# Smaller MLP tiles in a fused recurrent-attention and MLP kernel: two chunk-batches per tile, attention stages respaced over three PSUM slots, loads reordered

## The chip, the core and the metric

The kernel runs on one core of a Trainium2 chip. The metric is the device time of one execution in microseconds (us), as the median of several runs. Engines are named as in the profile: PE is TensorE's matmul stream and PEld its weight loads, DVE is VectorE, ACT is ScalarE, POOL is GpSimd, and SP is SyncE, whose queue here issues every DMA.

## The reference

The first half is a linear attention with a decaying state for 4 batches, 8 heads, 768 steps and head dimension 48. The second half is an MLP on the 3072 rows of 384 that come out of it.

```
state = 0
for t in range(768):
    cur      = einsum('bhd,bhe->bhde', u * k[t], v[t])
    y[t]     = einsum('bhd,bhde->bhe', r[t], state + cur)
    state    = w[t][..., None] * state + einsum('bhd,bhe->bhde', k[t], v[t])
x = y.transpose(0, 2, 1, 3).reshape(3072, 384)
h = x @ w_in                       # 384 -> 2048
g = s * relu(h)**2 + b
out = g @ w_out                    # 2048 -> 384
```

## The kernel before

Time is cut into six chunks of 128 steps. One chunk of one batch is a *chunk-batch*, numbered n from 0 to 23: n // 4 is the chunk and n % 4 the batch. All work on 128 rows.

**Attention of one chunk-batch.** `load` brings w, r, k and v (four DMAs of 192 KB). ACT takes the logarithm of w (`ln`, L127). PE turns it into running sums with triangular matrices (`cum`, L169 to L177), ACT exponentiates them (`expo`, L191 and L195), and DVE multiplies r and k by them (`mult`, L201, tile prd). PE transposes prd (`trans`, L228, tile trps), and the evacuation out of PSUM is shared: DVE copies one half (L244, RT), ACT the other (L245, KTr). PE forms the matrix of the chunk (`mt`, L255), DVE masks it (`mask`, L267). PE makes the state's increment (`dmm`, L308, tile d_ps) and the output (`ymm`, L283 and L292, tile y_ps). DVE adds increment and state (`supd`, L349, tile stmp) and POOL scales the sum (L352). DVE adds the diagonal term to y_ps (`yevac`, L322), PE transposes the result (`xtr`, L364) and ACT copies it into xT (`xevac`, L379). POOL makes the diagonal term's parts beside this (`pool1` L132, L139 and L144, `pool2` L156), with a reduction on DVE between them (`cdiag`, L150).

**MLP.** A tile T is one chunk of all four batches, so 512 tokens and six tiles. `g1` makes 128 hidden rows for 512 tokens with three matmuls of 512 columns (L413); `relu` on ACT (L426) and `square` on DVE (L431) follow. `g2` makes a quarter of the output of 128 tokens with four matmuls of 384 columns (L446); after four of them `oevac` on DVE (L456) scales and an output DMA follows (L465). One such g1 or g2 step is called a *unit* below; both halves of the MLP have 96 units in g1 and 96 in g2.

**Order.** The schedule is manual: each call gets a number (key), the calls are sorted by it, and each engine executes its instructions in that order. `base(n)` spaces chunk-batches 4 keys apart, 2 for the first four; the stages of chunk-batch n have fixed offsets from it. SP issues the loads in that order too, and each load waits for a free buffer.

**PSUM.** The tiles trps, d_ps, y_ps and xt_ps rotate through pool psB with two slots; cums and mt_ps share one slot of two banks (psA); h_ps has three slots (psH) and o_ps one (psO).

Of the kernel before, what the change touches and what calls it, by code (L numbers as in the profile page):

```python
# [16 lines left out]
def kernel(  # L17
# [23 lines left out]
    N = B * NCH  # L41
    NT = NCH
    TOK = B * L
    NPIECE = 4
# [11 lines left out]
    psB = ctx.enter_context(  # L56
        tc.tile_pool(name="psB", bufs=2, space=bass.MemoryType.PSUM)
    )
    psH = ctx.enter_context(
        tc.tile_pool(name="psH", bufs=3, space=bass.MemoryType.PSUM)  # L60
    )
# [178 lines left out]
    def tevac(n):  # L240
        c = cb[n]
        RT = work.tile([128, HP, 128], BF16, name="RT", tag="RT")
        KT_ = work.tile([128, HP, 128], BF16, name="KTr", tag="KTr")
        nc.vector.tensor_copy(out=RT, in_=c["trps"][:, 0:HP, :])  # L244
        nc.scalar.copy(out=KT_, in_=c["trps"][:, HP : 2 * HP, :])  # L245
        c["RT"] = RT
        c["KT"] = KT_

# [26 lines left out]
    def ymm(n):  # L275
# [98 lines left out]
    def xevac(n):  # L374
        c = cb[n]
        cc, bb = coords(n)
        if bb == 0:
            xT[cc] = mlp.tile([128, KT, TOK], BF16, name="xT", tag="xT", bufs=2)
        nc.scalar.copy(  # L379
            out=xT[cc][:, :, bb * L : (bb + 1) * L], in_=c["xt_ps"]  # L380
        )

# [24 lines left out]

    def g1(T, ft):
        if ft == 0:
            gT[T] = mlp.tile([128, FT, TOK], BF16, name="gT", tag="gT", bufs=2)  # L410
        ps = psH.tile([128, TOK], FP32, name="h_ps", tag="h")
        for kt in range(KT):
            nc.tensor.matmul(  # L413
                ps,
                lhsT=w_in_sb[ft // FPP][
                    :, kt, (ft % FPP) * 128 : (ft % FPP + 1) * 128
                ],
                rhs=xT[T][:, kt, :],
                start=(kt == 0),
                stop=(kt == KT - 1),  # L420
            )
        hs[T, ft] = ps

    def relu(T, ft):
        rh = mlp.tile([128, TOK], BF16, name="rh", tag="rh", bufs=4)
        nc.scalar.activation(out=rh, in_=hs[T, ft], func=AF.Relu)  # L426
        hs[T, ft] = rh

    def square(T, ft):
        rh = hs.pop((T, ft))  # L430
# [51 lines left out]
    def at(key, fn, *a):  # L482
        ev.append((key, len(ev), fn, a))

    def base(n):
        return -24 + 2 * n if n < B else 4 * (n - B)

    for n in range(N):
# [10 lines left out]
        at(q + 5.00, tevac, n)  # L499
        at(q + 6.20, mt, n)  # L500
        at(q + 7.00, mask, n)
        at(q + 8.10, dmm, n)
        at(q + 8.30, supd, n)
        at(q + 8.20, ymm, n)
        at(q + 9.00, yevac, n)
        at(q + 10.20, xtr, n)
        at(q + 11.00, xevac, n)

    def g1key(T, i):
        return i if T == 0 else 24 + 16 * (T - 1) + i  # L510

    def g2key(T, i):
        return 17.5 + 1.4 * i if T == 0 else g1key(T, 15) + 2 + i

    for T in range(NT):
        for ft in range(FT):
            q = g1key(T, ft)
            at(q + 0.40, g1, T, ft)
            at(q + 0.45, relu, T, ft)
            at(q + 1.10, square, T, ft)  # L520
        for i in range(16):
# [81 lines left out]
```

## Time and profile before

| | us |
|---|---|
| median of three runs (281.06 to 281.78) | 281.51 |
| the profiled execution | 282.26 |
| its span, first to last instruction | 280.3 |
| PE busy | 192.6 (69%) |
| DVE busy | 169.2 (60%) |
| POOL busy | 123.4 (44%) |
| ACT busy | 109.4 (39%) |
| mean granted clock of TensorE | 0.976 |

The page gives busy times over the whole span. The stages of this kernel have different limits, so the stretches are read one by one: the first 40 us, in which loads arrive and the first four chunk-batches are worked on; a long stretch in which attention and MLP alternate at an even period; and an end in which only the MLP is left.

### The profile page before, as it was taken

The page shows a single profiled execution, that of the slowest core. Times are in us where ns is not written, and L with a number is a line of the kernel's source. Part 1 is how long each engine was busy: PE and PEld are TensorE (multiplying, and loading weights), DVE is VectorE, ACT ScalarE, POOL GpSimd, SP SyncE. Part 2 cuts the span into 40 slices and gives each one's busy share as a digit, 9 for nine tenths or more (in the row PEclk, how much of TensorE's full clock was granted, in tenths as well). Part 3 has the DMA queues.
Part 4 walks back from the last instruction along what each step waited for, and adds up shares of the span by engine and source line. Part 5 has one row for each costly group of instructions (what it writes and reads, how often), then busy time and mean ns, then how long its engine had stood idle before and what let it go on. Part 6 is the DMA issues. An engine that isn't in the chain of part 4 may idle for free.

```text
span 280.3 us, 4354 instructions
## 1 busy us (share of the span) xinstructions
PE 192.6 (69%) x1602; PEld 116.6 (42%) x1624; DVE 169.2 (60%) x270; ACT 109.4 (39%) x214; POOL 123.4 (44%) x150
## 2 busy tenths in 40 slices
PE   1233678354767676767675776776769779999994
PEld 0122543233444444444443444444445445545562
DVE  3333946767555576796677677677767685443421
ACT  3122236324514254536435434434444544444400
POOL 3654945967336753475446346347534510000000
PEclk9999999959879999999999999999999999999999
DMA  8999999999990529570707526616000000011021
GB/s 144 243 222 250 295 213 255 187 186 179 185 151 0 108 34 178 77 140 0 141 14 129 120 44 120 128 44 114 28 28 20 12 30 28 29 50 37 28 85 59
DMA packets 107462, 30.38 MB, mean 108 GB/s; under 512 B 100656, under 2 KB 105904, under 8 KB 107440
## 3 DMA queue, kind: packets, MB, share of 16 engines
q1 hardware_dynamic: 107440, 30.09, 53.1%
q8 instruction: 13, 0.21, 0.3%
q14 instruction: 9, 0.07, 0.1%
HBM read 25.36 MB, written 4.72 MB: 107 GB/s over the span
## 4 chain that ended last, share of the span: by engine, by line
PE 35%; DVE 24%; issue 12%; SPq 9%; ACT 9%; DMA 5%; POOL 3%; DVEq 0%; ACTq 0%; POOLq 0%
PE o_ps L446 11%; PE h_ps L413 11%; SPq L120 8%; DVE prd L201 7%; DVE gT L431 6%; DMA rkt<-in_k_dram 5%; PE trps L228 4%; ACT E L191 4%; DVE o_sb L456 4%; PE o_psh L446 4%; ACT rh L426 4%; DVE stmp L349 3%; PE mt_ps L255 3%; DVE x_sb L322 2%; DVE mt_sb L267 2%
## 5 line engine op out<-in xcount | busy, mean ns | idle before, releaser
L426 ACT ACTIVATE rh<-h_ps 128x512 bf16<-128x512 f32 x96 | 57.4, 598 | 101.5 <-PE h_ps L413 95.5
L413 PE MATMUL h_ps<-xT,w_in 128*128 128x512 bf16 x266 | 76.4, 394 | 1.9 <-ACT xT L379 0.6
L431 DVE TENSOR_TENSOR gT<-rh 128x512 bf16<-128x512 bf16 x96 | 57.7, 613 | 32.4 <-ACT rh L426 32.3
L446 PE MATMUL o_ps<-w_out,gT 128*128 128x384 bf16 x320 | 64.9, 326 | 1.8 <-DVE o_sb L456 0.7
L446 PEld LDWEIGHTS <-gT 128*128 128x128 bf16 x384 | 37.1, 98 | 34.9 <-issue 3.9
L228 PE MATMUL trps<-identity,prd 128*128 128x128 bf16 x192 | 17.5, 244 | 30.6 <-DVE stmp L349 28.1
L267 DVE TENSOR_TENSOR mt_sb<-mt_ps,tri_strict 128x1024 bf16<-128x1024 f32 x24 | 29.3, 1222 | 15.1 <-PE mt_ps L255 15.1
L413 PEld LDWEIGHTS <-w_in 128*128 128x128 bf16 x288 | 25.7, 100 | 21.9 <-issue 3.6
L132 POOL TENSOR_TENSOR rkp<-rkt 128x384 f32<-128x384 f32 x24 | 25.2, 1049 | 18.4 <-DMA rkt<-in_k_dram 18.4
L139 POOL TENSOR_TENSOR rku<-rkp,u_bc 128x384 f32<-128x384 f32 x24 | 31.7, 1320 | 2.9 <-DMA u_bc<-in_u_dram 1.1
L201 DVE TENSOR_TENSOR prd<-rkt,E 128x768 bf16<-128x768 f32 x24 | 29.4, 1227 | 0.3 <-ACT E L191 0.3
L215 POOL TENSOR_TENSOR l<-lam,par 128x8 f32<-128x8 f32 x20 | 4.9, 246 | 54.2 <-ACT lam L195 54.2
L456 DVE SCALAR_TENSOR_TENSOR o_sb<-o_ps,s_bc,bconst 128x384 f32<-128x384 f32 x20 | 12.3, 616 | 26.5 <-PE o_ps L446 26.5
L228 PEld LDWEIGHTS <-prd 128*128 128x128 bf16 x192 | 14.3, 109 | 32.6 <-issue 28.2
L255 PE MATMUL mt_ps<-RT,KTr 48*128 48x128 bf16 x192 | 10.4, 231 | 25.2 <-ACT lam L195 18.6
L156 POOL TENSOR_TENSOR yd<-vt,cd 128x384 bf16<-128x384 f32 x24 | 20.2, 841 | 15.5 <-DVE cd L150 15.4
L245 ACT COPY KTr<-trps 128x512 bf16<-128x512 bf16 x24 | 14.0, 582 | 29.1 <-DVE RT L244 29.1
L150 DVE TENSOR_REDUCE cd<-rku 128x8 f32<-128x384 f32 x24 | 13.1, 547 | 19.7 <-POOL rku L139 19.7
L169 PE MATMUL cums<-logw,tri_strict 128*128 128x384 bf16 x24 | 9.2, 384 | 17.4 <-ACT logw L127 17.4
L191 ACT ACTIVATE E<-cums 128x768 bf16<-128x768 f32 x24 | 19.4, 810 | 3.1 <-PE cums L177 3.0
L255 PEld LDWEIGHTS <-KTr 48*128 48x128 bf16 x192 | 7.7, 99 | 27.5 <-issue 21.3
L352 POOL TENSOR_TENSOR st<-stmp,l 128x384 bf16<-128x384 bf16 x16 | 13.3, 828 | 11.9 <-DVE stmp L349 11.9
(46 smaller groups left out, 198.0 us busy)
## 6 DMA issues: line engine op xcount, KB each, us to landing
wt<-in_w_dram SPq DMA_DIRECT2D x24, 192.0 KB, 4.4
rkt<-in_r_dram SPq DMA_DIRECT2D x24, 192.0 KB, 4.2
rkt<-in_k_dram SPq DMA_DIRECT2D x24, 192.0 KB, 4.5
vt<-in_v_dram SPq DMA_DIRECT2D x24, 192.0 KB, 4.4
out_dram<-o_sb SPq DMA_DIRECT2D x24, 192.0 KB, 1.9
wi_st<-in_moe_w_in_dram SPq DMA_DIRECT2D x4, 768.0 KB, 6.8
wo_st<-in_moe_w_out_dram SPq DMA_DIRECT2D x4, 768.0 KB, 6.4
u_bc<-in_u_dram SPq DMA_DIRECT2D x1, 192.0 KB, 4.5
```

The costliest lines, as they stand in the source:

```text
L132: nc.gpsimd.tensor_tensor(out=rkp, in0=c["rk"][:, 0].rearrange("t h d -> t (h d)"), in1=c["rk"][:, 1].rearrange("t h d -> t (h d)"), op=AL ...
L139: nc.gpsimd.tensor_tensor(out=rku.rearrange("t h d -> t (h d)"), in0=rkp, in1=u_bc, op=ALU.mult)
L191: nc.scalar.activation(out=E, in_=ps[:, :, 0:HD], func=AF.Exp)
L201: nc.vector.tensor_tensor(out=prd[:, :, :, 0:D].rearrange("t x h d -> t (x h) d"), in0=c["rk"].rearrange("t x h d -> t (x h) d"), in1=c["E ...
L228: nc.tensor.matmul(ps[:, x * HP + p, :], lhsT=c["prd"][:, x, 2 * p : 2 * p + 2, :].rearrange("t h d -> t (h d)"), rhs=identity, is_transpo ...
L255: nc.tensor.matmul(ps[:, sg, p, :], lhsT=c["KT"][pr, p, :], rhs=c["RT"][pr, p, :], start=(p == 0), stop=(p == HP - 1),)
L267: nc.vector.tensor_tensor(out=m.rearrange("s g p t -> s (g p) t"), in0=c["mt_ps"].rearrange("s g p t -> s (g p) t"), in1=tri_strict.unsque ...
L413: nc.tensor.matmul(ps, lhsT=w_in_sb[ft // FPP][:, kt, (ft % FPP) * 128 : (ft % FPP + 1) * 128], rhs=xT[T][:, kt, :], start=(kt == 0), stop ...
L426: nc.scalar.activation(out=rh, in_=hs[T, ft], func=AF.Relu)
L431: nc.vector.tensor_tensor(out=gT[T][:, ft, :], in0=rh, in1=rh, op=ALU.mult)
L446: nc.tensor.matmul(ps, lhsT=gT[T][:, ft, tt * 128 : (tt + 1) * 128], rhs=w_out_sb[ft // FPP][:, ft % FPP, :], start=(ft == 0), stop=(ft == ...
L456: nc.vector.scalar_tensor_tensor(out=o_sb, in0=os_.pop((T, tt)), scalar=s_bc, in1=bconst, op0=ALU.mult, op1=ALU.add,)
```

## The change

An MLP tile becomes two chunk-batches (256 tokens), so there are twelve. A unit of g1 now makes 256 hidden rows for 256 tokens: six matmuls of 256 columns into one bank. psB gets three slots and psH two. ACT copies both halves of the transposed tile in one instruction (tile RK), and DVE's copy goes. The offsets of the attention stages change (dmm comes ahead of mt, ymm and xtr later), an 8-key hold stands before chunk-batch 6, and the g2 units of the first two tiles are placed behind it. ymm reads the state that supd put aside. Loads of the first chunk-batches come first, then w_in, then two chunk-batches, then w_out. xT and gT get three buffers.

```diff
+    CPT = 2
+    NT = N // CPT
+    TOK = CPT * L
+    FPQ = 512 // TOK
+    NQ = FT // FPQ
...
-        tc.tile_pool(name="psB", bufs=2, space=bass.MemoryType.PSUM)
+        tc.tile_pool(name="psB", bufs=3, space=bass.MemoryType.PSUM)
...
-        tc.tile_pool(name="psH", bufs=3, space=bass.MemoryType.PSUM)
+        tc.tile_pool(name="psH", bufs=2, space=bass.MemoryType.PSUM)
...
-        nc.vector.tensor_copy(out=RT, in_=c["trps"][:, 0:HP, :])
-        nc.scalar.copy(out=KT_, in_=c["trps"][:, HP : 2 * HP, :])
+        RK = work.tile([128, 2 * HP, 128], BF16, name="RK", tag="RK")
+        nc.scalar.copy(out=RK, in_=c["trps"])
...
-            st = states[bb]
+            st = c["st_in"]
...
+        ps = psH.tile([128, FPQ, TOK], FP32, name="h_ps", tag="h")
+        for f in range(FPQ):
+            ft = i * FPQ + f
+            for kt in range(KT):
+                nc.tensor.matmul(
+                    ps[:, f, :],
+                    lhsT=w_in_sb[ft // FPP][
+                        :, kt, (ft % FPP) * 128 : (ft % FPP + 1) * 128
+                    ],
+                    rhs=xT[T][:, kt, :],
+                    start=(f == 0 and kt == 0),
+                    stop=(f == FPQ - 1 and kt == KT - 1),
+                )
...
+    HOLD = 8
+
     def base(n):
-        return -24 + 2 * n if n < B else 4 * (n - B)
+        if n < B:
+            return -24 + 2 * n
+        return 4 * n - 16 + (HOLD if n >= B + CPT else 0)
...
-        at(q + 6.20, mt, n)
...
+        at(q + 6.70, dmm, n)
+        at(q + 7.20, mt, n)
...
     def g1key(T, i):
-        return i if T == 0 else 24 + 16 * (T - 1) + i
+        return 1 + 8 * T + (HOLD if T >= 3 else 0) + i
...
     def g2key(T, i):
-        return 17.5 + 1.4 * i if T == 0 else g1key(T, 15) + 2 + i
+        if T < 2:
+            return 24.6 + 4 * T + 0.5 * i
+        return g1key(T + 1, 0) + i
...
-    order = [(load, 1), (load_win, 0), (load, 2), (load_win, 1), (load, 3)]
-    order += [(load_win, 2), (load_win, 3), (load_wout, 0), (load_wout, 1)]
-    order += [(load, 4), (load_wout, 2), (load_wout, 3), (load, 5), (load, 6)]
-    order += [(load, 7)]
+    order = [(load, 1), (load, 2), (load, 3)]
+    order += [(load_win, i) for i in range(NPIECE)]
+    order += [(load, 4), (load, 5)]
+    order += [(load_wout, i) for i in range(NPIECE)]
+    order += [(load, 6), (load, 7)]
...
-        at(-10 + i, cast_in, i)
-        at(1.05 + 3 * i, cast_out, i)
-    at(17.3, colsum)
+        at(-6 + i, cast_in, i)
+        at(9.05 + 2 * i, cast_out, i)
+    at(16.9, colsum)
```

The instructions are moved on every engine; three places matter below. The first is SP's queue near its start, before the change; wt is the first of a chunk-batch's four loads, wi_st a piece of w_in and wo_st a piece of w_out.

```order
L120 DMA wt_138<-in_w_dram 128x8x48
...
L386 DMA wi_st_145<-in_moe_w_in_dram 128x3x512
L120 DMA wt_147<-in_w_dram 128x8x48
...
L386 DMA wi_st_154<-in_moe_w_in_dram 128x3x512
L120 DMA wt_156<-in_w_dram 128x8x48
...
L386 DMA wi_st_163<-in_moe_w_in_dram 128x3x512
L386 DMA wi_st_165<-in_moe_w_in_dram 128x3x512
L396 DMA wo_st_167<-in_moe_w_out_dram 128x4x384
L396 DMA wo_st_169<-in_moe_w_out_dram 128x4x384
L120 DMA wt_171<-in_w_dram 128x8x48
```

With the change the same queue reads:

```order
L123 DMA wt_138<-in_w_dram 128x8x48
...
L123 DMA wt_145<-in_w_dram 128x8x48
...
L123 DMA wt_152<-in_w_dram 128x8x48
...
L386 DMA wi_st_159<-in_moe_w_in_dram 128x3x512
...
L386 DMA wi_st_165<-in_moe_w_in_dram 128x3x512
L123 DMA wt_167<-in_w_dram 128x8x48
...
L123 DMA wt_174<-in_w_dram 128x8x48
...
L396 DMA wo_st_181<-in_moe_w_out_dram 128x4x384
```

Chunk-batches 1 to 3 now come without a weight piece between them. Chunk-batch 4 had four pieces of w_in and two of w_out ahead of it, and now has the four of w_in alone.

The second place is PE in the even stretch, before the change (the first matmul of each group):

```order
L308 MATMUL d_ps<-vb,prd_105 128x96
...
L283 MATMUL y_ps<-st_1502,RT 128x96
...
L292 MATMUL y_ps<-vb,mt_sb 128x48
...
L228 MATMUL trps<-identity,prd_106 128x128
...
L413 MATMUL h_ps<-xT,w_in_97 128x512
...
L446 MATMUL o_ps<-w_out_101,gT 128x384
...
L169 MATMUL cums<-logw_104,tri_strict 128x384
```

With the change:

```order
L309 MATMUL d_ps<-vb,prd_107 128x96
...
L256 MATMUL mt_ps<-RK 128x128
...
L415 MATMUL h_ps<-xT,w_in_97 128x256
...
L366 MATMUL xt_ps<-identity,x_sb 128x128
...
L448 MATMUL o_ps<-w_out_100,gT 128x384
...
L231 MATMUL trps<-identity,prd_105 128x128
...
L415 MATMUL h_ps<-xT,w_in_97 128x256
```

Before, d_ps and y_ps take both slots of psB just ahead of trps, which so needs d_ps's slot back; now trps stands five groups behind d_ps, and its slot is that of the y_ps before.

The third place is DVE in the even stretch, one period before the change:

```order
L244 COPY RT<-trps 128x512
L431 TENSOR_TENSOR gT<-rh 128x512
L150 TENSOR_REDUCE cd<-rku 128x8
L431 TENSOR_TENSOR gT<-rh 128x512
L267 TENSOR_TENSOR mt_sb<-mt_ps,tri_strict 128x1024
L201 TENSOR_TENSOR prd_107<-rkt,E 128x16x48
L431 TENSOR_TENSOR gT<-rh 128x512 x2
L349 TENSOR_TENSOR stmp<-d_ps,st_1251 128x384
L456 SCALAR_TENSOR_TENSOR o_sb<-o_ps,s_bc,bconst 128x384
L322 TENSOR_TENSOR x_sb<-y_ps,yd 128x384
```

With the change:

```order
L153 TENSOR_REDUCE cd<-rku 128x8
L433 TENSOR_TENSOR gT<-rh 128x512
L323 TENSOR_TENSOR x_sb<-y_ps,yd 128x384
L204 TENSOR_TENSOR prd_105<-rkt,E 128x16x48
L433 TENSOR_TENSOR gT<-rh 128x512
L351 TENSOR_TENSOR stmp<-d_ps,st_1538 128x384
L268 TENSOR_TENSOR mt_sb<-mt_ps,tri_strict 128x1024
L433 TENSOR_TENSOR gT<-rh 128x512
L458 SCALAR_TENSOR_TENSOR o_sb<-o_ps,s_bc,bconst 128x384
L433 TENSOR_TENSOR gT<-rh 128x512
```

RT's copy is gone, the mask stands behind prd and stmp instead of ahead of them, and the squares are spread singly over the period.

## Rows read from the trace of the kernel before

**Rows 1.** Windows: stretch, busy us of each engine, granted clock, DMA share, GB/s.

```profile
core 0: us, PE busy (x) PEld busy (x) DVE busy (x) ACT busy (x) POOL busy (x), PEclk, DMA share, GB/s
60.95:81.08 20.13, 12.06 (x109) 7.62 (x110) 13.73 (x21) 8.72 (x19) 10.20 (x13) 0.84 1.28 186
158.33:168.71 10.38, 7.38 (x68) 4.57 (x69) 7.23 (x11) 4.43 (x10) 5.01 (x6) 1.00 0.49 96
217.98:226.52 8.54, 6.95 (x60) 4.24 (x61) 6.43 (x10) 4.36 (x10) 4.13 (x5) 1.00 0.06 23
234.95:265.96 31.01, 30.54 (x175) 16.07 (x175) 13.83 (x30) 13.99 (x25) 0.00 (x0) 1.00 0.09 33
```

**Rows 2.** Chain that ended last, one even period: start us, us, what.

```profile
158.33 0.70 ACT E L191
...
163.72 0.48 DVE stmp L349
...
164.23 0.61 PE trps L228 x8
...
166.18 0.62 DVE o_sb L456
...
168.71 0.70 ACT E L191
```

**Rows 3.** Waits over the whole span: us in total, times, longest.

```profile
PE trps L228 <- DVE stmp L349: 28.1, 16, 4.3
```

**Rows 4.** Groups by line, 130 to 200 us: busy us, mean ns, idle before.

```profile
L431 DVE TENSOR_TENSOR gT<-rh 128x512 bf16<-128x512 bf16 x28 | 19.1, 698 | 3.2 <-ACT rh L426 3.2
L139 POOL TENSOR_TENSOR rku<-rkp,u_bc 128x384 f32<-128x384 f32 x7 | 11.1, 1593 | 0.5
L201 DVE TENSOR_TENSOR prd<-rkt,E 128x768 bf16<-128x768 f32 x7 | 8.5, 1209 | 0.0
L132 POOL TENSOR_TENSOR rkp<-rkt 128x384 f32<-128x384 f32 x7 | 7.0, 1000 | 0.0
L413 PEld LDWEIGHTS <-w_in 128*128 128x128 bf16 x81 | 6.7, 97 | 4.9
L352 POOL TENSOR_TENSOR st<-stmp,l 128x384 bf16<-128x384 bf16 x7 | 5.8, 829 | 6.0 <-DVE stmp L349 6.0
L191 ACT ACTIVATE E<-cums 128x768 bf16<-128x768 f32 x7 | 5.7, 815 | 0.0
L245 ACT COPY KTr<-trps 128x512 bf16<-128x512 bf16 x7 | 4.1, 585 | 9.0 <-DVE RT L244 9.0
L244 DVE COPY RT<-trps 128x512 bf16<-128x512 bf16 x7 | 2.9, 416 | 0.2 <-PE trps L228 0.2
```

**Rows 5.** Timeline, arrivals: logarithms of chunk-batches 2, 3 and 4 on ACT.

```profile
16.05 0.52 ACT L127 ACTIVATE logw<-wt 128x384 bf16<-128x384 f32 x1 [4.64 <-DMA wt<-in_w_dram]
22.91 0.52 ACT L127 ACTIVATE logw<-wt 128x384 bf16<-128x384 f32 x1 [4.43 <-DMA wt<-in_w_dram]
39.60 0.53 ACT L127 ACTIVATE logw<-wt 128x384 bf16<-128x384 f32 x1
```

**Rows 6.** Timeline, PE and POOL: chunk-batches 4, 5 and the last start, colsum.

```profile
40.98 0.53 PE L169 MATMUL cums<-logw,tri_strict 128*128 128x384 bf16 x1
48.82 0.99 POOL L132 TENSOR_TENSOR rkp<-rkt 128x384 f32<-128x384 f32 x1 [2.25 <-DMA rkt<-in_k_dram]
81.08 3.37 PE L470 MATMUL cs_ps<-w_out,ones 128*128 128x384 bf16 x16
223.79 0.33 PE L169 MATMUL cums<-logw,tri_strict 128*128 128x384 bf16 x1
```

**Rows 7.** Chain that ended last, its end: start us, us, what.

```profile
262.72 0.65 PE h_ps L413 x3
...
265.96 10.41 PE o_psh L446 x64
...
276.40 0.62 DVE o_sb L456
```

More of the change, by code (lines that the diff above doesn't have):

```diff
@@ L41 @@
     N = B * NCH
-    NT = NCH
-    TOK = B * L
+    CPT = 2
[3 more added lines that the diff above has]
+    NQ = FT // FPQ
     NPIECE = 4
@@ L241, in tevac @@
         c = cb[n]
-        RT = work.tile([128, HP, 128], BF16, name="RT", tag="RT")
-        KT_ = work.tile([128, HP, 128], BF16, name="KTr", tag="KTr")
-        nc.vector.tensor_copy(out=RT, in_=c["trps"][:, 0:HP, :])
-        nc.scalar.copy(out=KT_, in_=c["trps"][:, HP : 2 * HP, :])
-        c["RT"] = RT
-        c["KT"] = KT_
+        RK = work.tile([128, 2 * HP, 128], BF16, name="RK", tag="RK")
+        nc.scalar.copy(out=RK, in_=c["trps"])
+        c["RT"] = RK[:, 0:HP, :]
+        c["KT"] = RK[:, HP : 2 * HP, :]
     def mt(n):
@@ L332, in supd @@
         cc, bb = coords(n)
+        c["st_in"] = states[bb]
         if cc == NCH - 1:
@@ L375, in xevac @@
         c = cb[n]
[L376 to L381, printed above, removed]
+        T, j = divmod(n, CPT)
+        if j == 0:
+            xT[T] = mlp.tile([128, KT, TOK], BF16, name="xT", tag="xT", bufs=3)
+        nc.scalar.copy(out=xT[T][:, :, j * L : (j + 1) * L], in_=c["xt_ps"])
     def load_win(i):
@@ L406, with g1, relu, square @@
     hs = {}
[L408 to L430, printed above, removed]
+    def g1(T, i):
+        if i == 0:
+            gT[T] = mlp.tile([128, FT, TOK], BF16, name="gT", tag="gT", bufs=3)
+        ps = psH.tile([128, FPQ, TOK], FP32, name="h_ps", tag="h")
[11 more added lines that the diff above has]
+                )
+        hs[T, i] = ps
+    def relu(T, i):
+        rh = mlp.tile([128, FPQ, TOK], BF16, name="rh", tag="rh", bufs=4)
+        nc.scalar.activation(out=rh, in_=hs[T, i], func=AF.Relu)
+        hs[T, i] = rh
+    def square(T, i):
+        rh = hs.pop((T, i))
         nc.vector.tensor_tensor(
-            out=gT[T][:, ft, :], in0=rh, in1=rh, op=ALU.mult
+            out=gT[T][:, i * FPQ : (i + 1) * FPQ, :], in0=rh, in1=rh, op=ALU.mult
         )
@@ L463, in oevac @@
         )
-        row0 = tt * S + T * L
+        cc, bb = coords(T * CPT + tt)
+        row0 = bb * S + cc * L
         nc.sync.dma_start(out=out[row0 : row0 + 128, :], in_=o_sb)
@@ L499 @@
         at(q + 5.00, tevac, n)
-        at(q + 6.20, mt, n)
[L501 to L507, printed above, removed]
+        at(q + 6.70, dmm, n)
+        at(q + 7.20, mt, n)
+        at(q + 7.50, supd, n)
+        at(q + 8.00, mask, n)
+        at(q + 9.70, ymm, n)
+        at(q + 10.50, yevac, n)
+        at(q + 11.50, xtr, n)
+        at(q + 12.00, xevac, n)
     def g1key(T, i):
-        return i if T == 0 else 24 + 16 * (T - 1) + i
+        return 1 + 8 * T + (HOLD if T >= 3 else 0) + i
     def g2key(T, i):
-        return 17.5 + 1.4 * i if T == 0 else g1key(T, 15) + 2 + i
+        if T < 2:
+            return 24.6 + 4 * T + 0.5 * i
+        return g1key(T + 1, 0) + i
     for T in range(NT):
[L516 to L521, printed above, removed]
+        for i in range(NQ):
+            q = g1key(T, i)
+            at(q + 0.40, g1, T, i)
+            at(q + 0.45, relu, T, i)
+            at(q + 1.10, square, T, i)
+        for i in range(4 * CPT):
             q = g2key(T, i)
@@ L567 @@
     for n in range(8, N):
-        at(base(n) - 14.5, load, n)
+        at(base(n) - 22.5, load, n)
     ev.sort(key=lambda e: (e[0], e[1]))
```

## The prediction

> **What bounds the kernel now.** I read the windows first, because the busy shares of the page mix stages. In the even stretch one chunk-batch takes 10.38 us, and in it PE is busy 7.38, DVE 7.23, POOL 5.01 and ACT 4.43 [rows 1]. No engine is full, so an order of waits sets the period. The chain of waits shows it as a ring: E on ACT, then mt, mask and prd, stmp on DVE, the transposes trps on PE, two MLP units, o_sb on DVE, trps's evacuation, and E of the next chunk-batch 10.38 us later [rows 2]. The link that need not be there is stmp to trps: the reader should see in the sum of waits that PE stood 28.1 us, 16 times, before trps until DVE's stmp had given d_ps's slot of psB back [rows 3]. Where this wait is gone by itself (chunk-batches 20 to 22 have no state update), the period is 8.54 [rows 1].
>
> After the last attention PE is the bound: busy 30.54 of 31.01 us [rows 1], at 0.65 us for an MLP unit [rows 7]. That end is long, because a tile of 512 tokens waits for its fourth chunk-batch: from the last chunk-batch's running sums at 223.79 [rows 6] to 280.3 are 56.5 us. At the front, arrivals set the pace: ACT's logarithms of chunk-batches 2, 3 and 4 start at 16.05, 22.91 and 39.60 [rows 5].
>
> **The change part by part.**
>
> *Loads.* With c for a chunk-batch's loads and p for a weight piece, 22.91 - 16.05 = c + p = 6.86 and 39.60 - 22.91 = c + 4p = 16.69 [rows 5], so p is 3.3 us. Chunk-batch 3 loses two pieces ahead of it, and so does chunk-batch 4; both come 6.6 us earlier. The work between them moves with them, so the running sums of chunk-batch 4 move from 40.98 [rows 6] to 34.4. The bounds are no gain (41) and this one. Chunk-batch 5 loses four pieces and arrives before it is wanted; chunk-batch 6 has the same bytes ahead of it as before, one c (3.6) behind the 48.82 at which chunk-batch 5 was there [rows 6], so about 52.4.
>
> *Keys 1 to 17.* Here stand 16 g1 units and the attention of chunk-batches 4 and 5. DVE is the fullest engine. Of its 7.23 us per chunk-batch, four squares are 4 x 0.698, o_sb 0.62 and RT 0.42 [rows 1, 4, 7]; 3.4 are left for attention. So 16 x 0.698 + 2 x 3.4 = 18.0 us. PE needs 16 x 0.65 + 2 x 2.2 = 14.8 (2.2 is 7.38 less eight units of 0.65). The column sums follow, 3.4 us [rows 6], and the running sums of chunk-batch 6 start at 34.4 + 18.0 + 3.4 = 55.8, after its arrival. The bounds are 52 with PE as the limit, and 62 if PE runs this stage at the mixed clock that it had at 60.95 to 81.08, 0.84 [rows 1].
>
> *The even stretch.* The third slot and the new offsets cut the ring: trps now takes the slot of a y_ps whose x_sb was made well before it. DVE loses RT's copy, 7.23 - 0.42 = 6.8. ACT copies 1024 columns in one instruction: 0.585 for 512 and 0.815 for 768 [rows 4] give 0.9 ns a column and 1.05 us, so ACT has 4.43 - 0.59 + 1.05 = 4.9. That is no bound, and the copy lies behind a relu and ahead of a mt that comes two units later; its cover is ACT's idle half. A g1 unit has as many columns as before. I follow one period by hand in the new order of PE: running sums 0.4, then units, y_ps, d_ps, mt, xt and trps. E is ready before mt, prd before trps, the mask before the next running sums, and o_sb runs while PE does running sums and one g1 unit (1.1 us against 0.62 plus hand-over). Nothing stalls PE, so the floor is PE's 7.38. The next ring is 7.9: on DVE cd, a square, x_sb, prd, a square, stmp, then on POOL st, rkp and rku, and back to cd. With 0.48 for each short DVE step [rows 2], 2 x 0.698, 1.209, 0.829, 1.000 and 1.593 [rows 4] it is 7.5, and nine hand-overs of about 0.05 make it 7.9. But rku's 1.593 is a price beside busy squares, and cd may come late by 0.5 without anyone waiting, so I take 7.6, nearer to PE's floor. The bounds are 7.38 and the 8.54 of rows 1.
>
> Two chunk-batches (6, 7) have g1 units and no g2, for which I keep 7.6; two (8, 9) have eight g2 units, whose single o_ps slot is handed back twice in a period behind DVE's queue, 0.3 us each: 8.2. Chunk-batch 10 starts at 55.8 + 15.2 + 16.4 = 87.4, and chunk-batch 23, thirteen periods on, at 87.4 + 13 x 7.6 = 186.2.
>
> *The end.* From there PE's order has 20 g1 and 28 g2 units and about 1.5 chunk-batches of attention: 48 x 0.65 + 1.5 x 2.2 = 34.5 us. o_sb and the last output DMA stay, 280.3 - 276.4 = 3.9 [rows 7]. Six hand-backs of the o_ps slot, each 0.62 for o_sb and 0.2 around it less the g1 unit of 0.65 that covers it, make 1.1. Together 39.5, where it was 56.5.
>
> *Edits at nothing.* psH with two slots: a relu of 512 columns costs about what ACT's copy of 512 does, 0.585 [rows 4], and a slot is wanted again two units (1.3 us) later at the earliest; without that cover PE would wait 0.6 per unit. Six narrow matmuls for three wide ones: the weight loads hide, see below. The hold: its keys are filled with MLP units that had to be done anyhow. The output DMAs: same count and size.
>
> *Sum.* 186.2 + 39.5 = 225.7 us of span. The profiled execution of before took 282.26 for a span of 280.3, so 227.7; it lies 0.75 above the median of its runs, which is less than what I know. **228.0 us.**
>
> [...] PE had a granted clock of 1.00 in the even stretch at 7.38 busy of 10.38, and 0.84 at 60.95 to 81.08, where it was busy 12.06 of 20.13 [rows 1]. [...]
>
> **The rivals.**
>
> 1. *The period stays near 8.54.* For it: that period is the only one measured without the stmp wait [rows 1], and DVE works in order with 6.8 of 7.6 us filled, so one late mask delays all behind it. Against: in that stretch mask still stood ahead of prd. Time: 13 x 0.94 and four times 0.5 more, 242.
>
> 2. *The new order of loads brings nothing at the front.* If the drain of the first four chunk-batches, not the arrivals, ends last, chunk-batch 4 starts at 41 as before: 6.6 more, 234.5. For it: one DVE works off four chunk-batches there in order. Against: ACT waited 4.64 and 4.43 us for the loads themselves [rows 5].
>
> 3. *The clock falls.* [...] Against: clock 1.00 wherever PE was busy over 70% [rows 1].
>
> 4. *Weight loads stand in line, and it is slower.* A g1 unit now has six loads for six matmuls of 256 columns. If such a matmul no longer covers its load of 97 ns [rows 4], 576 loads cost 55.9 us where PE is the bound: 284. From 93 ns exposed per load on, the gain is gone. Against: eight 128-column transposes, each with its own load, end in 0.61 us [rows 2], so loads hide under half this width. [...]
>
> **How the numbers follow.** The forecast has 0.60, rival 1 has 0.25, rival 2 has 0.09, rivals 3 and 4 have 0.03 each. The forecast's own range, from PE's floor in all periods with a fast front (7.38 and 52: 228 less 2.9, 3.8 and 1) to a period of 8.0 with a front at 58, is 220 to 236. With rivals 1 and 2, and rival 1 with a front two to four us late, it reaches to 246. A run can tell about 0.3% from no change, 0.85 us. Faster takes the first three and the clock, 0.97; of rival 4, 0.02 lie above 282.4 and 0.01 between.
>
> **What would show it.** Right: no wait of trps on stmp worth naming; PE busy over 90% in the middle; DVE without RT, ACT's copy at about 1.05; chunk-batch 4's sums at 34 to 35, chunk-batch 23's near 186, 40 us behind them; mean time of g1 matmuls about 0.11 us from start to start. Wrong: a period over 8.2 with PE waiting in one place every period, above all for DVE's o_sb or mask or for POOL through cd; a granted clock well under 1.00 after 60 us; chunk-batch 4 at 40.

## The result, and the profile after

The changed kernel takes 226.36 us (median of four runs, 226.26 to 227.96) where the kernel before took 281.64 beside it: ratio 0.806, 95% interval 0.802 to 0.810. Medians are over all runs, while the ratios leave out two slow ones, 286.08 of the kernel before and 245.72 of the new order alone, without which these two medians would be 281.51 and 242.88. The forecast was 228.0. The profiled execution is the slowest of the changed kernel: it took 227.96 for a span of 226.0, where its other runs have spans of 224.3 to 225.2. Its mean granted clock is 0.955. The sum was right; its terms were not all right, and that is what the experiments are about.

The page's busy line of after, then the tenths of PE in 40 slices and the granted clock in them:

```profile
PE 189.2 (84%) x1912; PEld 141.1 (62%) x1912; DVE 163.1 (72%) x246; ACT 119.3 (53%) x214; POOL 126.2 (56%) x150
...
PE   1253649874919798999999999999999999999992
...
PEclk9999955999785999999999999999999999999999
```

Below are windows of after. Each begins with the first running-sum matmul (cums) of a chunk-batch: 4, 6, 8, 10, 11 and 23.

```profile
core 0: us, PE busy (x) PEld busy (x) DVE busy (x) ACT busy (x) POOL busy (x), PEclk, DMA share, GB/s
0.00:33.12 33.12, 13.38 (x149) 10.15 (x150) 17.18 (x30) 13.03 (x22) 22.92 (x34) 0.93 1.02 220
33.12:60.67 27.55, 21.81 (x195) 16.26 (x195) 20.41 (x27) 14.20 (x26) 19.43 (x19) 0.84 1.13 238
60.67:77.26 16.59, 10.54 (x90) 7.76 (x88) 6.88 (x12) 8.26 (x17) 7.49 (x9) 0.79 1.23 179
77.26:93.02 15.76, 14.69 (x147) 9.66 (x147) 11.02 (x15) 6.41 (x12) 9.47 (x13) 1.00 1.07 187
93.02:100.26 7.24, 7.24 (x83) 5.62 (x82) 6.50 (x9) 3.80 (x8) 5.05 (x7) 1.00 0.61 128
100.26:186.50 86.24, 86.24 (x954) 66.56 (x953) 82.14 (x119) 58.05 (x106) 60.97 (x69) 1.00 0.44 94
186.50:226.00 39.50, 35.34 (x304) 25.09 (x302) 18.98 (x37) 15.58 (x27) 0.83 (x1) 1.00 0.11 41
```

From 93 us to its last matmul, 35.3 us into the last window, PE has no gap: 7.24 busy of 7.24 per chunk-batch, where it was 7.38 of 10.38 [rows 1]. The loss has moved to the front: between 33 and 77 us PE is busy 32.4 of 44.1 us, at granted clocks of 0.84 and 0.79.

One period of after in the chain of waits is PE alone (start us, us, what):

```profile
122.13 0.16 PE cums L172
...
122.54 0.68 PE h_ps L415 x6
123.21 0.65 PE o_ps L448 x4
...
125.54 0.17 PE d_ps L309 x4
125.71 0.33 PE mt_ps L256 x8
126.04 0.76 PE h_ps L415 x6
...
127.62 0.45 PE trps L231 x8
```

The ring of [rows 2] is gone, and so is the wait of [rows 3]. What PE still waits for in the whole span is at the front (us in total, times, longest):

```profile
PE cums L172 <- ACT logw L130: 11.9, 4, 4.8
PE xt_ps L366 <- DVE x_sb L323: 6.7, 4, 3.0
PE h_ps L415 <- ACT rh L428: 4.6, 1, 4.6
PE cums L172 <- DVE mt_sb L268: 4.5, 2, 3.9
...
PE trps L231 <- DVE prd L204: 0.5, 2, 0.3
```

Two of these were not foreseen. The first is in ACT's timeline:

```profile
66.00 0.58 ACT L480 ACTIVATE bconst<-cs_ps,b_bc 128x384 f32<-128x384 f32 x1 [7.93 <-DMA b_bc<-in_moe_b_dram]
66.48 0.59 ACT L428 ACTIVATE rh<-h_ps 128x512 bf16<-128x512 f32 x1
```

`bconst` (the column sums of w_out times the bias b) reads b_bc, a small load that stands on SP behind the loads of chunk-batches 8 and 9. The column sums used to come at 81 us [rows 6]; now they are done at 60.8, and b_bc is not there: SP issues it at 62.9, and it lands 3.0 us later. Of ACT's 7.93 idle us the first 2.8 pass before the column sums are done, and the other 5.2 are b_bc's. ACT works in order, so the relu behind bconst waits too, and PE waits 4.56 us for that relu.

The second is on DVE, beside POOL's casts of w_out (first two rows from POOL's timeline, the others from DVE's):

```profile
44.80 1.46 POOL L540 CAST w_out<-wo_st 128x1536 bf16<-128x1536 f32 x1
46.20 1.66 POOL L540 CAST w_out<-wo_st 128x1536 bf16<-128x1536 f32 x1
```

```profile
44.89 1.64 DVE L433 TENSOR_TENSOR gT<-rh 128x512 bf16<-128x512 bf16 x1
46.46 1.68 DVE L433 TENSOR_TENSOR gT<-rh 128x512 bf16<-128x512 bf16 x1
48.39 0.55 DVE L323 TENSOR_TENSOR x_sb<-y_ps,yd 128x384 bf16<-128x384 f32 x1
48.86 0.41 DVE L433 TENSOR_TENSOR gT<-rh 128x512 bf16<-128x512 bf16 x1
```

The square at 48.86, with no POOL instruction beside it, takes 0.41 us, and the two that start beside these casts take 1.64 and 1.68; two later casts lengthen two more squares to 1.61 and 1.68. x_sb of chunk-batch 5 started only at 55.06, PE waited 3.05 us for it, and the granted clock was half just behind that wait (0.50 from 55.7 to 58 us; the column sums took 3.60 us).

### The profile page after: what moved, and what is told of

It reads as the page before. It is cut to its first block, busy times and chain, and to the rows that moved or that the text cites. A ratio compares the mean times of both kernels' runs of the same rounds, so it can differ in the third digit from the quotient of the medians.

```text
span 226.0 us, 4923 instructions
## 1 busy us (share of the span) xinstructions
PE 189.2 (84%) x1912; PEld 141.1 (62%) x1912; DVE 163.1 (72%) x246; ACT 119.3 (53%) x214; POOL 126.2 (56%) x150
## 4 chain that ended last, share of the span: by engine, by line
PE 70%; DVE 8%; ACT 3%; issue 2%; SPq 2%; DMA 1%; ACTq 0%
PE o_ps L448 26%; PE h_ps L415 26%; PE trps L231 4%; DVE gT L433 3%; PE mt_ps L256 3%; PE o_psh L448 2%; DVE o_sb L458 2%; PE xt_ps L366 2%; PE y_ps L293 2%; PE cums L172 2%; PE y_ps L284 1%; PE cums L175 1%; DMA b_bc<-in_moe_b_dram 1%; SPq L123 1%; ACT rh L428 1%
## 5 line engine op out<-in xcount | busy, mean ns | idle before, releaser
L428 ACT ACTIVATE rh<-h_ps 128x512 bf16<-128x512 f32 x96 | 57.3, 599 | 56.1 <-PE h_ps L415 53.4
L415 PE MATMUL h_ps<-xT,w_in 128*128 128x256 bf16 x576 | 81.6, 283 | 4.6 <-ACT rh L428 4.6
L433 DVE TENSOR_TENSOR gT<-rh 128x512 bf16<-128x512 bf16 x96 | 67.2, 705 | 24.5 <-ACT rh L428 24.2
L448 PE MATMUL o_ps<-w_out,gT 128*128 128x384 bf16 x352 | 70.9, 326 | 1.3 <-DVE o_sb L458 1.1
L415 PEld LDWEIGHTS <-w_in 128*128 128x128 bf16 x576 | 53.5, 101 | 15.1 <-issue 4.7
L159 POOL TENSOR_TENSOR yd<-vt,cd 128x384 bf16<-128x384 f32 x24 | 29.2, 1215 | 5.8 <-DVE cd L153 5.7
L142 POOL TENSOR_TENSOR rku<-rkp,u_bc 128x384 f32<-128x384 f32 x24 | 25.9, 1080 | 3.0 <-DMA u_bc<-in_u_dram 1.2
L246 ACT COPY RK<-trps 128x1024 bf16<-128x1024 bf16 x24 | 24.2, 1007 | 2.0 <-PE trps L231 2.0
L153 DVE TENSOR_REDUCE cd<-rku 128x8 f32<-128x384 f32 x24 | 13.1, 544 | 16.4 <-POOL rku L142 16.4
L204 DVE TENSOR_TENSOR prd<-rkt,E 128x768 bf16<-128x768 f32 x24 | 24.1, 1005 | 1.1 <-ACT E L194 0.8
L172 PE MATMUL cums<-logw,tri_strict 128*128 128x384 bf16 x24 | 8.8, 368 | 16.4 <-ACT logw L130 11.9
L381 ACT COPY xT<-xt_ps 128x384 bf16<-128x384 bf16 x24 | 11.4, 475 | 17.1 <-PE xt_ps L366 17.1
L130 ACT ACTIVATE logw<-wt 128x384 bf16<-128x384 f32 x24 | 12.7, 530 | 8.2 <-DMA wt<-in_w_dram 8.2
```

Source lines behind the costliest of these rows:

```text
L142: nc.gpsimd.tensor_tensor(out=rku.rearrange("t h d -> t (h d)"), in0=rkp, in1=u_bc, op=ALU.mult)
L159: nc.gpsimd.tensor_tensor(out=yd, in0=c["v"], in1=c["cd"].unsqueeze(2).to_broadcast([128, H, D]), op=ALU.mult,)
L204: nc.vector.tensor_tensor(out=prd[:, :, :, 0:D].rearrange("t x h d -> t (x h) d"), in0=c["rk"].rearrange("t x h d -> t (x h) d"), in1=c["E ...
L246: nc.scalar.copy(out=RK, in_=c["trps"])
L415: nc.tensor.matmul(ps[:, f, :], lhsT=w_in_sb[ft // FPP][:, kt, (ft % FPP) * 128 : (ft % FPP + 1) * 128], rhs=xT[T][:, kt, :], start=(f == ...
L428: nc.scalar.activation(out=rh, in_=hs[T, i], func=AF.Relu)
```

## The experiments

The kernels ran on several chips, the kernel before beside each. Medians and ratios to before are given. Differences to the changed kernel are given as a range of two figures, by medians and by ratios times 281.6.

This table, worked out from the traces, gives the start of the first cums of chunk-batches 4, 6, 10 and 23, and the span, in us:

| kernel | 4 | 6 | 10 | 23 | span |
|---|---|---|---|---|---|
| before | 41.0 | 61.0 | 98.0 | 223.8 | 280.3 |
| after | 33.1 | 60.7 | 93.0 | 186.5 | 226.0 |
| two slots | 34.5 | 63.0 | 90.8 | 184.2 | 223.8 |
| before, three slots | 40.3 | 59.0 | 90.7 | 201.4 | 258.0 |
| new order alone | 39.3 | 70.7 | 96.7 | 186.4 | 241.9 |
| split evacuation | 34.5 | 62.1 | 92.4 | 186.2 | 225.7 |
| old loads | 38.2 | 69.2 | 95.6 | 189.1 | 228.6 |
| tile of four | 33.2 | 60.2 | 89.8 | 179.4 | 234.8 |
| biases early | 33.2 | 61.7 | 88.1 | 181.5 | 221.1 |
| casts on ACT | 33.0 | 57.6 | 91.4 | 184.9 | 224.4 |
| both | 33.4 | 57.8 | 84.2 | 177.7 | 217.2 |
| both, loads of 4 first | 33.2 | 61.6 | 88.0 | 181.5 | 221.0 |
| both, tile of one | 36.9 | 60.2 | 89.3 | 183.6 | 215.3 |
| the same, chunk-batch 4 early | 30.3 | 62.1 | 91.2 | 185.5 | 217.4 |

Each row is one execution. That of after lies 1.6 us above the median of its runs, so small differences between rows count for little.

### What cut the ring: the third slot, or the order?

The prediction named both in one sentence. Two runs take them apart.

```diff
-        tc.tile_pool(name="psB", bufs=3, space=bass.MemoryType.PSUM)
+        tc.tile_pool(name="psB", bufs=2, space=bass.MemoryType.PSUM)
...
-        tc.tile_pool(name="psH", bufs=2, space=bass.MemoryType.PSUM)
+        tc.tile_pool(name="psH", bufs=3, space=bass.MemoryType.PSUM)
```

**The changed kernel with two slots.**

Expected, before it ran:

> The changed kernel with the PSUM slots of the old kernel (two for the big tiles, three for the hidden tiles), the new order of stages kept. Theory A (the new offsets alone take the trps-on-stmp wait out of the period: stmp's last read lies about 5.1 us into the period of 7.24, the next trps is wanted at about 5.5): period 7.2 to 7.5 us, time 226 to 230. Theory B (two slots tie trps to the state's last read again): period 8.5 us or more, 13 periods add 17 us or more, time 242 or more.

226.33 us (225.15 to 227.32), ratio 0.802 (0.797 to 0.806): not told apart from the changed kernel. The period stays at PE's floor:

```profile
134.20:141.40 7.20, 7.20 (x82) 5.61 (x81) 6.85 (x11) 4.81 (x10) 5.15 (x7) 1.00 0.71 140
```

So with the new order the third slot is worth nothing that can be measured.

**The kernel before with three slots.** The same edit the other way round, in the old order.

Expected, before it ran:

> The kernel before with one edit: three PSUM slots for the big tiles and two for the hidden tiles, its own order of stages. Theory B (the slot alone breaks the ring of waits): its periods fall from about 10.2 us to 8.5 us, 16 of them give 25 us, time 253 to 260. Theory A (the offsets are what counts): the trps-on-stmp wait stays or turns into another, time within 3 us of 281.5.

258.16 us, ratio 0.916 (0.911 to 0.921). In the old order the slot alone is worth 24 us. The wait of trps on stmp is gone, and the period is 8.8 us, near the 8.54 that the prediction read from the stretch without that wait. Another ring is left, and the wait in it is this:

```profile
PE mt_ps L255 <- ACT lam L195: 21.1, 16, 1.9
```

Its chain (start us, us, what):

```profile
140.72 0.62 DVE o_sb L456
141.34 0.46 DVE x_sb L322
141.80 0.34 DVE RT L244
...
142.65 0.60 ACT rh L426
143.25 0.70 ACT E L191
...
144.07 0.40 PE mt_ps L255 x8
```

E and lam (the exponentials on ACT) come late because the evacuation of the transposes and a relu stand ahead of them, and mt, the next thing PE has to do, needs them. The period is the one that rival 1 named, but not by its reason: the wait is for lam on ACT, and DVE's mask is not in the chain.

**The new order alone.** The changed kernel with its other four parts undone: tile of four, two slots, split evacuation, old loads (the edits are those shown with the single runs; the third xT buffer and the new keys of the later loads and of the casts stay).

Expected, before it ran:

> The changed kernel with four of its five parts undone together: tiles of four chunk-batches, two PSUM slots, the split evacuation, the old load order. What is left is the new order of stages. If the parts add up (226.4 + 10.8 for the tile + 5.0 for the loads + 1 for the evacuation + 0 for the slots), 241 to 245, so that the new order alone is worth 37 to 41 us of the 55. Rival (each part alone is covered by the others; without the third slot and with the long tile the old wait comes back): 250 or more, with a wait of trps on stmp of over 10 us.

243.32 us, ratio 0.856 (0.851 to 0.860), as added up from the other runs. The order (with its hold and the state put aside for ymm) alone takes PE to 57.34 busy of 57.40 us from chunk-batch 15 to 23:

```profile
129.00:186.40 57.40, 57.34 (x533) 34.48 (x531) 53.32 (x87) 35.08 (x70) 40.35 (x45) 1.00 0.31 70
```

This is the largest part by far, 38 to 41 of the 55 us. Such shares hang on what is there already: the third slot is worth 24 us in the old order and nothing in the new one. Which piece of the order (the offsets, the hold, the state put aside, the keys of the loads) carries it was not tried apart.

### The other parts of the change

**Split evacuation.**

Expected, before it ran:

> The changed kernel with the evacuation of the transposes split as before (the r half on VectorE, the key half on ScalarE), all else kept. Theory (TensorE's 7.24 us bound the period; VectorE goes from 6.3 to about 6.7 us of it, still below): within 1 us of 226.4, period 7.2 to 7.3. Rival (VectorE in order is late for the mask and with it for TensorE): period 7.6 or more, 13 periods add 5 us, time 231 or more.

```diff
-        RK = work.tile([128, 2 * HP, 128], BF16, name="RK", tag="RK")
-        nc.scalar.copy(out=RK, in_=c["trps"])
+        nc.vector.tensor_copy(out=RT, in_=c["trps"][:, 0:HP, :])
+        nc.scalar.copy(out=KT_, in_=c["trps"][:, HP : 2 * HP, :])
```

227.42 us, ratio 0.806 (0.801 to 0.810): the same as the changed kernel within what can be told. DVE had the room: from chunk-batch 11 to 23 it is busy 79.1 of 86.5 us, and PE all of them.

**Old load order.**

Expected, before it ran:

> The changed kernel with the loads in the old order. Theory of the prediction (first cums of chunk-batch 4 waits for the load: 6.6 us later): first cums of chunk-batch 4 at 40 to 41, time 232 to 234. Rival (the later stalls of the front, for b_bc and the squares, take the delay in): 226 to 229.

```diff
-    order = [(load, 1), (load, 2), (load, 3)]
-    order += [(load_win, i) for i in range(NPIECE)]
...
+    order = [(load, 1), (load_win, 0), (load, 2), (load_win, 1), (load, 3)]
+    order += [(load_win, 2), (load_win, 3), (load_wout, 0), (load_wout, 1)]
...
```

231.32 us, ratio 0.817 (0.812 to 0.823): the new order of loads is worth 3 to 5 us, not 6.6. The result lies between the two expectations, and chunk-batch 4 starts at 38.2 instead of 40 to 41. The table shows why the gain shrinks. Chunk-batch 6 starts 8.5 us later than in the changed kernel, but chunk-batch 10 only 2.6. With the old loads the column sums come so late that bconst (at 69.42) no longer waits for b_bc, and chunk-batch 6 takes 4.7 us instead of 10.3. The changed kernel loses there most of what its loads win.

**Tile of four.** The loads, slots, evacuation and attention offsets stay.

Expected, before it ran:

> The changed kernel with MLP tiles of four chunk-batches (512 columns), all else kept (loads, slots, evacuation, attention offsets). Theory (the small tile's gain is the shorter work behind the last cums): work after the last cums 52 to 56 us instead of 39.5, period a little under 7.24, time 236 to 242. Rival (the small tile costs TensorE as much by its extra weight loads as it gives back at the end): 224 to 229.

```diff
-    CPT = 2
+    CPT = 4
...
-        return 1 + 8 * T + (HOLD if T >= 3 else 0) + i
+        return 1 + i if T == 0 else 33 + 16 * (T - 1) + i
```

(g2's first tiles and gT's buffers go with it.) 237.15 us, ratio 0.838 (0.833 to 0.842). The small tile is worth 9 to 11 us, as expected. The last cums come earlier here, at 179.4, since more MLP work is left over; the end behind them is 55.4 us against 39.5.

### The two stalls at the front

**Biases early.**

Expected, before it ran:

> The changed kernel with one DMA group moved: the two loads of the small biases (s_bc, b_bc) go out ahead of the w_out rows instead of behind the loads of chunk-batches 8 and 9. Theory (ScalarE's bconst waits 7.9 us for b_bc, relu behind it keeps TensorE waiting 4.6 us, and the clock then starts from half): the 4.6 us go and some of the cold stretch with them, first cums of chunk-batch 10 at about 87 to 89 instead of 93.0, time 220 to 222. Rival (the wait only covers squares and loads that are late anyway): within 1 us of 226.4.

```diff
-    at(6.03, small)
+    at(-51.5, small)
```

221.96 us, ratio 0.786 (0.780 to 0.791): 4 to 6 us gained, as expected. bconst starts at 61.89, right behind the column sums; chunk-batch 10 is at 88.1.

**Casts on ACT.**

Expected, before it ran:

> The changed kernel with the float32 to bfloat16 casts of w_out on ScalarE instead of GpSimd. Theory (the GpSimd casts run beside VectorE's squares, which take 1.2 to 1.45 us there instead of 0.42 and make x_sb of chunk-batch 5 late; TensorE waited 3.1 us for it and fell to half clock): squares near 0.45 us, first cums of chunk-batch 10 at 88 to 90 instead of 93.0, time 221 to 224. Rival (ScalarE's own casts, four of 1.3 to 1.5 us, come ahead of relu and give it back): within 1 us of 226.4 or slower.

```diff
-        nc.gpsimd.tensor_copy(out=w_out_sb[i], in_=w_out_st[i])
+        nc.scalar.copy(out=w_out_sb[i], in_=w_out_st[i])
```

226.54 us, ratio 0.800 (0.796 to 0.804): no gain that can be told, and yet the mechanism is there. PE's waits from chunk-batch 6 to 10 say where the gain went:

```profile
PE h_ps L415 <- ACT rh L428: 6.8, 1, 6.8
```

Chunk-batch 6 starts 3.1 us earlier, and then PE waits 6.8 us for the relu behind bconst instead of 4.6: b_bc comes hardly earlier, and bconst starts at 65.2 where it was 66.0. (The 1.2 to 1.45 us of the expectation are means over three squares each, one of which ran behind the casts.) Expectation missed; the rival's result came, but not by the rival's reason.

**Both.**

Expected, before it ran:

> The changed kernel with both edits of the front: small biases loaded ahead of the w_out rows, casts of w_out on ScalarE. If the two stalls are separate, their gains add: first cums of chunk-batch 10 at 83 to 86, time 215 to 219. Rival (one late item, the arrival of the chunk-batches, stands behind both): no better than the better of the two alone, 220 to 222.

219.05 us (218.51 to 219.21), ratio 0.773 (0.769 to 0.777): at the upper end of the 215 to 219 expected. Once b_bc is there, the casts are worth 2.9 to 3.6 us more. Squares from 39.1 to 57.8 us take 470 ns in the mean; in after, from 39.1 to 60.7, they took 965 (groups by line, both first, then after):

```profile
L433 DVE TENSOR_TENSOR gT<-rh 128x512 bf16<-128x512 bf16 x14 | 6.5, 470 | 6.2 <-ACT rh L428 6.2
```

```profile
L433 DVE TENSOR_TENSOR gT<-rh 128x512 bf16<-128x512 bf16 x13 | 12.2, 965 | 2.2 <-ACT rh L428 2.2
```

With the two long waits gone, the granted clock of this run is 1.00 from 33 to 93 us. The two gains do not simply add: alone they are 4 to 6 us and about nothing, together 7 to 9. They are two stalls in a row on one path, where the later one hides the earlier.

### How narrow can a tile be?

**Tile of one.** On top of both edits.

Expected, before it ran:

> The version with both stalls removed, with MLP tiles of one chunk-batch: a unit of the first product is twelve matmuls of 128 columns, each with its own weight load. If a 128-column matmul with its load takes the 76 ns that eight transposes of that width show, a unit takes 0.91 instead of 0.65 us, four per chunk-batch make the period 8.2 to 8.4, time 236 to 242. Rival 4 of the prediction, here at its strongest (load of 97 ns and matmul in line): unit 1.8 us, time over 300. If the loads still hide entirely: 215 to 218.

```diff
-    CPT = 2
+    CPT = 1
...
-        return 1 + 8 * T + (HOLD if T >= 3 else 0) + i
+        return 4 * T - 3 + (HOLD if T >= 6 else 0) + i
...
-        if T < 2:
-            return 24.6 + 4 * T + 0.5 * i
+        if T < 4:
+            return 20.8 + 2 * T + 0.5 * i
```

(xT and gT get six and seven of the smaller buffers.) 217.23 us (217.06 to 217.46), ratio 0.766 (0.763 to 0.768): the fastest kernel of this study. The theory of 236 to 242 fell, and the last case came: the loads hide even under 128 columns. The chain shows g1 units at 0.67 us with twelve weight loads each:

```profile
127.10 0.65 PE o_ps L448 x4
...
128.12 0.67 PE h_ps L415 x12
128.80 0.65 PE o_ps L448 x4
```

The period is 7.30 against 7.24, so six more weight loads in each of the four g1 units cost 0.06 us together. The end behind the last cums falls from 39.5 to 31.7. Of these 7.8 us, 5 are given back at the front (chunk-batch 10 at 89.3 instead of 84.2) and 0.8 in thirteen longer periods. Of the 5, 3.5 are there at chunk-batch 4 already: its logarithm on ACT now stands behind three relus of the first tiles and starts at 36.34 instead of 32.78.

### Two tries on the front that failed

In after, chunk-batch 4's cums are not held up by the load. ACT's timeline has its logarithm right behind the copies into xT of the first chunk-batches, with no wait for a DMA:

```profile
32.16 0.48 ACT L381 COPY xT<-xt_ps 128x384 bf16<-128x384 bf16 x1 [1.05 <-PE xt_ps L366]
32.54 0.53 ACT L130 ACTIVATE logw<-wt 128x384 bf16<-128x384 f32 x1
```

**Loads of chunk-batch 4 ahead of the last two pieces of w_in.**

Expected, before it ran:

> The version with both stalls removed (small biases early, casts of w_out on ScalarE) and the loads of chunk-batch 4 moved ahead of the last two pieces of w_in. Theory (the front is set by arrivals, TensorE idle for 19 of the first 33 us): first cums of chunk-batch 4 at 27 instead of 33.4, and 2 to 4 us of it are left at the end, 215 to 217. Rival (the first MLP units then wait for the last pieces of w_in and hold up the chunk-batches behind them in order): 219 to 222.

```diff
-    order += [(load_win, i) for i in range(NPIECE)]
-    order += [(load, 4), (load, 5)]
+    order += [(load_win, 0), (load_win, 1), (load, 4)]
+    order += [(load_win, 2), (load_win, 3), (load, 5)]
```

222.68 us, ratio 0.784 (0.780 to 0.787), slower than without it. Chunk-batch 4 starts at 33.2 as before, for the reason above. And POOL, in order too, now waits for the late pieces of w_in before it makes chunk-batch 4's products:

```profile
33.02 1.47 POOL L537 CAST w_in<-wi_st 128x1536 bf16<-128x1536 f32 x1 [5.02 <-DMA wi_st<-in_moe_w_in_dram]
35.16 1.47 POOL L537 CAST w_in<-wi_st 128x1536 bf16<-128x1536 f32 x1 [0.67 <-DMA wi_st<-in_moe_w_in_dram]
36.59 0.99 POOL L135 TENSOR_TENSOR rkp<-rkt 128x384 f32<-128x384 f32 x1
```

DVE's cd and prd of chunk-batch 4 stand behind rkp, and PE waits 3.15 us for prd.

**The first stages of chunk-batch 4 moved up as well,** on the tile of one.

Expected, before it ran:

> The version with tiles of one chunk-batch, with the first stages of chunk-batch 4 moved ahead of the drain of the first four: its loads before the last two pieces of w_in, its logarithm on ScalarE ahead of the copies into xT, its running sums ahead of the last output stages of chunk-batch 3, its GpSimd products ahead of the last two casts of w_in, and its later stages some four to six keys earlier. Theory (the running sums of chunk-batch 4 wait since the change in ScalarE's order, not for a load: the logarithm stands behind the xT copy of chunk-batch 3, and in the run that only moved loads behind GpSimd's casts): they start at 29 to 31 instead of 36.9, and 2 to 4 us are left at the end, 213 to 215. Rival (TensorE and VectorE make up the idle time before chunk-batch 10 anyway, or the last pieces of w_in come late): 216.5 or more.

```diff
+        if n == B:
+            at(-11, ln, n)
+            at(-8.4, cum, n)
+            at(-8.35, expo, n)
+            at(-4.5, pool1, n)
...
```

219.18 us, ratio 0.777 (0.775 to 0.778): the step did what it said, and the kernel is slower than without it, as the rival had it. Chunk-batch 4 starts at 30.3 instead of 36.9, but chunk-batch 6 at 62.1 instead of 60.2. Two things are in the rows. The granted clock was 0.57 just behind the start, with PE having waited for x_sb, and from 42 to 62 us PE was busy only 14.0 of 20.0:

```profile
30.30:36.00 5.70, 4.99 (x57) 4.39 (x55) 3.08 (x4) 2.50 (x6) 4.31 (x6) 0.57 1.21 288
...
42.10:62.10 20.00, 13.98 (x204) 11.77 (x204) 13.46 (x22) 14.98 (x23) 6.74 (x8) 1.00 1.11 228
```

In the latter stretch it waited 2.8 us for relus, which alternate on ACT with the four 1.5 us casts of w_out, 2.0 for x_sb and 1.3 for prd. How much of the loss each makes was not tried apart and stays open.

## Why the prediction was right, step by step

| step | forecast | measured | off by |
|---|---|---|---|
| cums of chunk-batch 4 | 34.4 | 33.1 | -1.3 |
| keys 1 to 17 with the column sums | 21.4 | 27.55 | +6.2 |
| chunk-batches 6 and 7 | 15.2 | 16.6 | +1.4 |
| chunk-batches 8 and 9 | 16.4 | 15.8 | -0.6 |
| thirteen periods | 98.8 | 93.5 | -5.3 |
| the end | 39.5 | 39.5 | 0.0 |
| span | 225.7 | 226.0 | +0.3 |

The forecast (PE becomes the bound of the even stretch, the end shrinks by 17 us) is what happened, but that the sum came out to 0.3 us is luck: two errors of 5 to 6 us cancelled, and the measured column is the slowest run, 0.8 to 1.7 us of span above the others.

**"The cums of chunk-batch 4 move to 34.4."** The number held and the reason only in part. I took the work between load and cums as moving along with the load. It does so for the old loads (38.2 with them: w lands at 37.6 and the logarithm starts at 37.59), but with the new ones ACT's order ends last: 5.0 us of the 6.6 show at that point. The term also came from a row that does not show what I read in it. The third row of [rows 5] has no wait for a DMA: that w was issued at 31.2 and landed 6.8 us later, at 38.0, and its logarithm stood behind a copy into xT until 39.60:

```profile
39.22 0.48 ACT L379 COPY xT<-xt_ps 128x384 bf16<-128x384 bf16 x1 [1.80 <-PE xt_ps L364]
```

So 16.69 is not c + 4p alone, and p is not shown to be 3.3.

**"Keys 1 to 17 ... 18.0 us" and "the column sums follow, 3.4".** This step failed in size, 27.55 instead of 21.4, and in part in its bound. Chunk-batch 6 at 60.7 lies inside the bound of 62, but 62 does not follow from a clock of 0.84: 34.4 + 18.2 / 0.84 is 56.1. I took DVE as the limit and priced its squares at 0.698, a mean of squares with and without a POOL instruction beside them. Here POOL was casting w_out, and the 16 squares of this stage took 0.864 in the mean; I named the casts nowhere. The run with both edits needs 24.5 us, so 3.1 come back. The other 3.1 over the forecast are not DVE's. Its window in that run (columns as above) has DVE busy 14.3 us, less than I had put, and PE 20.2 where I had put 14.8 + 3.4:

```profile
33.35:57.84 24.49, 20.20 (x195) 15.19 (x194) 14.29 (x27) 18.81 (x30) 12.69 (x15) 1.00 1.09 242
```

The rest are waits of PE, the largest of them 2.6 us for relus on ACT. So with short squares DVE is not the limit of this stage; PE's own work and its waits in order are.

**"Two chunk-batches (6, 7) ... 7.6."** In length nearly right, in kind not: 4.6 us of it are the wait behind bconst. I followed the large loads on SP and left out the two small ones, whose reader the change moves from 81 to 61 us. The run with early biases shows their price, 4 to 6 us.

**"The floor is PE's 7.38."** This bound was too high: the period is 7.24. Busy time in the old kernel is not work. Added up, the chain of one period of after is eight units for 5.36 and 1.89 of attention, where I had taken 2.2. The eight transposes stand with 0.61 us in [rows 2] and with 0.45 in the packed chain. On the timelines of both kernels their records last 0.61 us, but in before the next h_ps starts 0.66 us behind their start (164.23 and 164.89), and in after 0.44 (127.46 and 127.90), while they still run. That such overlap makes up the difference in the period is my reading, not tested by a run of its own. "The next ring is 7.9" was too dear as well: rku, priced at 1.593, takes 1.14 in the mean from 100 to 186 us, and with PE full no such ring ends last.

**"The third slot and the new offsets cut the ring."** The new order does, of which the offsets are a part. Slots alone leave 8.8, the new order alone 7.2.

**"The end."** The total is exact, its terms are not: behind 186.5 PE waits for no o_sb, where I had put 1.1 us, its work is 35.3 instead of 34.5, and the tail behind its last matmul 4.2 instead of 3.9.

**"Edits at nothing."** The two h_ps slots and the weight loads held: no wait on relu in the even stretch. ACT's copy of both halves measured 1.007 against 1.05.

**The rivals.** Rival 1's period was seen only with the old order. Rival 2 fell in its number, since the old loads cost 3 to 5 us; but what it named, the drain of the first four chunk-batches, is what ends last ahead of chunk-batch 4 with the new loads. Rival 3 had a piece of truth, at the front alone: half clock in some slices behind PE's waits (0.50 from 67 to 70 us, behind the 4.56 us for the relu), so that one sign of being wrong did show (0.79 from 60.7 to 77.3 us). What I held against it, clock 1.00 wherever PE was busy over 70%, did not carry over: from 33.1 to 60.7 us PE was busy 21.8 of 27.6 us at 0.84. In the even stretch the granted clock is 1.00, with 256 columns (after, 93.0 to 186.5 us) and with 128 too (tile of one, 118.5 to 133.1). Rival 4 fell with the widest margin: twice its weight loads cost 0.06 us a period.

## What to carry to other kernels

When a change moves a stage earlier, list every input of every instruction in it, the smallest loads too, and find each on its queue; a load of 0.5 KB behind 1.5 MB on SP's queue held ACT back for 5.2 us and PE for 4.6. Look for the stall behind the stall before dropping an edit: the casts on ACT were worth nothing alone and 3 us with the biases early. And where a period is to be filled to one engine's floor, take that floor from the packed chain, not from busy time in a kernel with gaps.

## What the runs showed of the hardware

**DVE beside POOL.** A bfloat16 square, both operands in SBUF, took 0.41 us alone and 1.61 to 1.68 when it started beside a cast of w_out on POOL (after, 44.89 to 52.32). The casts come in pairs; the first of each took 1.46 and the second 1.66, and the casts of w_in with no square beside them 1.47 (in the run with the loads of chunk-batch 4 first). Two other instructions did not change: a reduction cd that started beside such a cast took 0.54 (kernel before, at 42.42; 0.55 in after at 58.45, with POOL idle), and RT's copy out of PSUM 0.42 (kernel before, at 59.91, where all 24 of them took 0.41 to 0.43). The square that starts at 44.89, 0.09 us behind a cast, ends at 46.53, 0.28 us behind the end of that cast. The other three end 0.27 or 0.28 us behind theirs, and each second cast, which starts while a square is still under way, is the longer one by 0.2. What holds the square back was not shown.

**Weight loads.** 396 loads of 97 ns each in the tile of one, from 100 to 160 us, take up only 22.6 us of PEld, so their records overlap one another, and twelve of them with twelve 128-column matmuls take 0.67 us, 56 ns a pair:

```profile
L415 PE MATMUL h_ps<-xT,w_in 128*128 128x128 bf16 x396 | 27.5, 219 | 0.0
...
L415 PEld LDWEIGHTS <-w_in 128*128 128x128 bf16 x396 | 22.6, 97 | 0.9
```

My own 76 ns, from eight transposes in 0.61, was too high: packed, the same eight take 0.45, which is 56 ns each.
